# Two-dimensional DFT and squared-ReLU block: a new plan for the side work of the first sequence, and two joins moved between the halves of a front

## The chip, the cores and the metric

The kernel runs on one core of one Trainium2 chip. The metric is the time of one execution in microseconds (us) on the device; lower is better. The engines are named as in the profile: PE is TensorE (matrix products), DVE is VectorE, ACT is ScalarE, POOL is GpSimd, SP is SyncE, which here only issues DMAs.

## The reference

```python
X = np.fft.fft(np.fft.fft(x, axis=1), axis=2).real   # x: 8 x 3008 x 256, float32
h = X.reshape(24064, 256) @ w_in                     # w_in: 256 x 2048
r = np.maximum(h, 0.0)
out = (r * r) @ w_out                                # w_out: 2048 x 256
```

So each of 8 sequences (b) of 3008 rows goes through a DFT over its rows and one over its 256 columns, of which the real part is kept, and then through two dense layers with a squared ReLU between.

## The kernel before

The column DFT is folded into w_in (G1, G2), so that the first layer reads the row DFT directly. By symmetry a sequence needs only 1505 frequencies: Pt and Qt hold the cosine and sine parts, and one pair of products gives hP and hQ, whose sum and difference are the first layer at a frequency and at its mirror. The frequencies are cut into 6 blocks of 252 (the last has 246), the hidden width into 8 pairs of slices (j = 0 to 7). One (block, j) is a **step**; a sequence has 48 steps, and steps are numbered through all 8 sequences (i, here mostly modulo 48).

In step i, in this order in the program:

- `front`: PE computes hP and hQ into two PSUM tiles of the pool "h", which has two buffers. DVE makes `he` from hP (two instructions, L1017), then g from he and hQ (L1019, L1020).
- `pending` work of a gathering, then **folds** and **composites** (below), then stores of results.
- the second layer for a pair of earlier steps, with fewer products by a Winograd-like scheme: an F group of 12 products (`first_half`, odd i) or an S group of 8 (`second_half`, even i). A product appears as two matmul instructions. Their operands are g and the 12 sums s, which POOL makes (L1039 to L1041 for even steps, L1049 to L1056 for odd ones).
- ACT's relu and square of g (L1024, L1027), and POOL's sums of it.

A block ends with a **gathering**: F and S products lie in six PSUM tiles (F0 to F2, S0 to S2), which DVE joins into the result c in `upper` and `lower` (one step after the last F group) and `joins` (two steps after, behind that step's front). S1 and S2 share a pool with two buffers, so the next block's S products can use S1's buffer only when the joins have read it.

Beside this, the row DFT of sequence b + 1 is computed while sequence b runs. It is a list of pieces with costs in us: **folds** (`fold_later`), which add and subtract mirrored rows and columns of x: R (rows), C (columns), both (parities), order (a shuffle), even and odd (butterflies), twice_even, twice_turned and twice_odd. Most copy one operand with ACT into a "spare" tile of the PSUM pool "h", so that DVE reads only one operand from SBUF; **composites** (`even` and `odd` of `dft_ops`), which are 8 small matmuls (pd, L743, L840, L866) into a tile of the same pool "h", put into an F or S group after its second product, and DVE joins of their halves. The column 128 of x for sequences 1 to 7 goes through its own small folds in the first sequence (`fold_columns`: begin, order, odd, even, odd_sums, twice_even, twice_odd) and its own composites (`dft_ops(None)`), whose result is stored to e_dram and read back in windows.

How the list is spread: in sequences 2 to 7 `pieces` takes up to two folds in a step, while their costs fit in ROOM[j] and the work is behind its due amount (`spent`, paced over the sequence); a composite goes into the step's F or S group when due (`piece_beside`). In the first sequence `first_pieces` does the same with CAPACITY and BESIDE, from a list that `ahead` and `woven` put together: folds, column work, table rearrangements (`part_table`) and composites in one order. Steps with j = 2 and 3 take none. The first sequence starts with a written-out order of tokens (ORDER) for its steps 0 to 9, in which the weights are still being prepared; the planner runs from step 10 (PLAIN) on.

x tiles are loaded by SP into three buffers, each next load issued by the fold R that frees one; the 56 small loads of column 128 (`load_columns`, L454) are issued six per step.

Of the kernel before, what the change touches and what calls it, by code (L numbers as in the profile page):

```python
# [84 lines left out]
def kernel(  # L85
# [321 lines left out]
    def make_turn():  # L407
        c, z = (turn[0:ROWS2, a, BY_AC:BY_AC + 1] for a in range(2))
        for a, (u, v, op) in enumerate(((c, z, ALU.add), (c, z, ALU.subtract), (z, c, ALU.subtract))):
            to = turn[0:ROWS2, a, BY_BD:BY_BD + 1]  # L410
            tt(out=to, in0=u, in1=v, op=op)
            nc.scalar.mul(to, to, 0.5 ** 0.5)

# [43 lines left out]

    def scale_columns():
        nc.scalar.mul(xe, xe, 2.0)

    def fold_columns():
# [12 lines left out]
        def begin():  # L474
            assert not COLUMNS
            scale_columns()
            s = hp.tile([P, 2, NL, NE], F32, name="es", tag="es", bufs=1)
            gt(out=s, in0=xe[:, 0::2], in1=xe[:, 1::2], op=ADD)
            for kp in range(2):
                gt(out=we[:, :, kp], in0=s[:, 0], in1=s[:, 1], op=SUB if kp else ADD)  # L480
# [9 lines left out]
        def even():  # L490
            nc.scalar.copy(a, we[r, first, 0])
            pair_up(we[r, first, 0], we[r, other, 0], a)
# [10 lines left out]
        def twice_even():  # L503
            nc.scalar.copy(one, we[r, 2:3, 0])
            for i, (u, k) in enumerate(((7, SIN), (5, LESS))):
                nc.scalar.mul(f[:, i], we[r, u, 0], by(BY_AB, k))
            for u in (5, 7):
                nc.scalar.mul(we[r, u, 0], we[r, u, 0], by(BY_AB, COS))
            pair_up(we[r, 2:3, 0], we[r, 4:5, 0], one)
            gt(out=we[r, 5:8:2, 0], in0=we[r, 5:8:2, 0], in1=f, op=ADD)  # L510

        def twice_odd():
            nc.scalar.copy(pair, we[r, v, 1])
            pair_up(we[r, v, 1], we[r, w, 1], pair)

        return [(0.1, begin), (0.3, order), (0.1, odd), (0.1, even), (0.1, odd_sums), (0.1, twice_even), (0.1, twice_odd)]

# [59 lines left out]
    def spare(r):  # L577


        return psh.tile([P, 2 * D], F32, name="sp", tag="h")[r]  # L580

    def fold_later(b):

# [11 lines left out]
        def rows_of(t):  # L595
            r = rows(t)

            def f():
                v, p, k = xt[b, t], spare(r).rearrange("p (i d) -> p i d", i=2), ordered.index(t)
                nc.scalar.copy(p, v[r, 1:3])  # L600
                if b == 1:
                    for u in ordered[k + (k > 0):k + 2]:
                        difference(u)
                fs[t] = next_sums()
                tt(out=fs[t][r, :, 0:D], in0=v[r, 0::3], in1=p, op=ADD)
                if b > 1:
                    fd[t] = fp.tile([P, 2, D], F32, name="fd", tag="fd")
                    tt(out=fd[t][r], in0=v[r, 0::3], in1=p, op=SUB)
                load_later(LATER.index((b, t)) + NX)

            return 0.7 if b == 1 else 1.3, f
# [89 lines left out]
        R, C, both = rows_of, columns_of, parities_of  # L701
        if b == 1:
            one = [R(TWO), R(TWO + 1), C(TWO), R(0), C(TWO + 1), both(TWO, TWO + 1), R(1), C(0), order(TWO + 1), C(1),
                   R(av), both(0, 1), even((TWO, TWO + 1)), odd(TWO, TWO + 1, BY_TWO)]
            two = [C(av), R(aw), R(bv), C(aw), both(av, aw), C(bv), order(aw), R(bw), even((av, aw)), odd(av, aw, BY_AC),
                   C(bw), both(bv, bw), order(bv), even((bv, bw)), odd(bv, bw, BY_BD)]
            return one, two + [(0.9, twice_even), (1.1, twice_turned), (1.4, twice_odd)]
# [295 lines left out]

    def front(b, k0, n, j):

# [9 lines left out]
        for h in range(2):  # L1015
            fc = j + NJ * h
            nc.vector.scalar_tensor_tensor(out=t[:, h, 0:n], in0=window[b, k0][:, 0:n], scalar=gE[:, fc:fc + 1],  # L1017
                                           in1=hP[:, h, 0:n], op0=ALU.mult, op1=ALU.add)
        tt(out=g[:, :, 0:n], in0=t[:, :, 0:n], in1=hQ[:, :, 0:n], op=ALU.add)  # L1019
        tt(out=g[:, :, n:2 * n][:, :, ::-1], in0=t[:, :, 0:n], in1=hQ[:, :, 0:n], op=ALU.subtract)  # L1020
# [95 lines left out]
    def gather(n, final):  # L1116
# [37 lines left out]
        def joins():  # L1154
            tt(out=o[:, 3::-2], in0=o[:, 3::-2], in1=S0[:, 0:2], op=ADD)
            tt(out=S0[:, 2], in0=S0[:, 2], in1=vt[:, 4], op=ADD)
            if not final:
                tt(out=S1[:, 1], in0=vt[:, 0], in1=S1[:, 1], op=SUB)
            tt(out=o[:, 2::3], in0=o[:, 2::3], in1=wide(S0[:, 2:3]), op=ADD)
            tt(out=o[:, 0], in0=o[:, 0], in1=S1[:, 2], op=ADD)  # L1160
            if not final:
                tt(out=o[:, 4], in0=o[:, 4], in1=S1[:, 1], op=ADD)

        return c, (early, upper, lower, back, joins)

# [41 lines left out]
    def ahead(b):  # L1207
        (_, start), *groups = dft_ops(b)
        tables = [(0.0, lambda tab=tab, t=t: part_table(tab, t)) for t in (TWO, ODD0) for tab in (cosT, sinT)]
        one, two = fold_later(b)  # L1210
        if b > 1:
            return one + two + [(0.0, start)] + groups
        head = [(0.0, start), *one[:3], (0.2, take_turn), *one[3:5], (0.5, make_turn), *one[5:9]]
        return (head + one[9:11] + woven(one[11:] + two[:5], fold_columns(), 1) + tables
                + woven(two[5:], dft_ops(None) + groups[0::2], 1) + groups[1::2])

    def woven(ops, others, each):

        out, others = [], list(others)
        for k in range(0, len(ops), each):  # L1220
            out += ops[k:k + each] + others[:1]
            del others[:1]
        return out + others

# [113 lines left out]
    per = len(BLOCKS) * NJ  # L1338
    side, spent, pace = [], 0.0, 0.0


    PLAIN = NJ + 2
    SHARE = (1.4, 2.3, 0.0, 0.0, 0.7, 1.6, 1.4, 1.6)
    FIRST = (1.6, 2.8, 0.0, 0.0, 0.9, 1.9, 1.6, 1.9)

    BESIDE = (2.2, 2.9, 0.0, 0.0, 1.7, 2.4, 2.2, 2.4)
    CAPACITY = (1.8, 2.8, 0.0, 0.0, 1.2, 2.2, 1.8, 2.2)
    ROOM = (1.6, 2.4, 0.0, 0.0, 1.0, 1.8, 1.6, 1.8)

    def share(i):  # L1350
        return 0.0 if i < PLAIN + 2 else FIRST[i % NJ] if i < per else SHARE[i % NJ]

    late = []

    def free_pieces():
        while late:
            late.pop(0)()
        while side and not side[0][0]:
            side.pop(0)[1]()
# [13 lines left out]

    def first_pieces(j):


        nonlocal spent
        room, hook = CAPACITY[j], None
        while side:
            t, f = side[0]  # L1380
            if spent + t / 2 > 0 or t > room + (0.6 if f in beside else 0.3) or f in beside and (hook or late):
                break
            if (f in beside or hook) and t + CAPACITY[j] - room > BESIDE[j]:
                break
            side.pop(0)
            if not t:
                late.append(f)
                continue
            spent, room = spent + t, room - t
            if f in beside:  # L1390
                hook = (2, f)
            else:
                f()
        return hook

    def piece_beside():
# [17 lines left out]
    ).split()  # L1414
    rounds = {"2": round_win(2, raw["in", 2])}
    loaded, freed = [], set()
    made = {}
# [20 lines left out]

    finished, pending = [], []

# [14 lines left out]
    def step(token):  # L1455
# [10 lines left out]
        elif what == "et":  # L1466
            made["et"]()
        elif what == "lc":
            load_columns(4)
# [42 lines left out]
    i = 0  # L1512
    spent, pace = 0.0, sum(t for t, _ in side) / sum(share(k) for k in range(per - 2))
    load_more()
    for token in ORDER:
        step(token)
    for i in range(PLAIN, len(steps) + 7):
        if i < len(steps):
            b, k0, n, j = steps[i]
            if i % per == 0:  # L1520
                assert not side
                side = ahead(b + 1) if b + 1 < B else []
                spent, pace = 0.0, sum(t for t, _ in side) / sum(share(i + k) for k in range(per - 2))
            if j == 2 and i + NJ < len(steps):
                load_window(*steps[i - 2 + NJ][:3])
            made["g", i] = g = front(b, k0, n, j)
            if i == PLAIN:
# [9 lines left out]
        if i < len(steps) and share(i):  # L1537
            spent -= pace * share(i) * (1.0 if i >= per else 1.08)
            if i < per:
                hook = first_pieces(j)  # L1540
            else:
                pieces()
                hook = (2, piece_beside)
# [5 lines left out]
        if at >= NJ and at < len(steps):  # L1549
            b_, k0_, n_, j_ = steps[at]  # L1550
            q = j_ // 2
            if not last_half:
                first_half(q, n_, made["g", at], made["g", at + 1], made["s", group], hook)
                if q == NJ // 2 - 1:
                    final = at + 2 == len(steps)
                    c_, ops = gather(n_, final)
                    gather_next = ops[0]
                    pending += [(i + 1, ops[1])] + ([] if final else [(i + 2, ops[3])]) + [(i + 2, ops[4])]
                    lower = (i + 1, ops[2])
                    finished += [(i + 3 + k if final else i + 4 + 2 * k, b_, k0_, n_, s_, c_, final)  # L1560
# [11 lines left out]
        free_pieces()  # L1572
        load_columns(6)


# [61 lines left out]
```

## Time and profile before

| | us |
|---|---|
| three runs | 1895.47, 1895.70, 1895.86 |
| median | 1895.7 |
| profiled execution | 1896.75 |
| its span, first to last instruction | 1895.0 |
| PE, DVE, POOL, ACT busy | 1865.4, 1474.3, 1465.5, 1082.3 |

The profile is of one execution. Busy time counts an engine's instructions, not its waits. A line of the view of waits names the waiting engine, tile and line, then what it waited for, then total us, times and the longest. A row of a timeline gives start, duration, engine, line, operation, output and inputs, shape and count, and in brackets the idle time before it and what ended it. The chain of waits follows the work that ended last back through the program.

### The profile page before, as it was taken

The page shows a single profiled execution, that of the slowest core. Times are in us where ns is not written, and L with a number is a line of the kernel's source. Part 1 is how long each engine was busy: PE and PEld are TensorE (multiplying, and loading weights), DVE is VectorE, ACT ScalarE, POOL GpSimd, SP SyncE. Part 2 cuts the span into 40 slices and gives each one's busy share as a digit, 9 for nine tenths or more (in the row PEclk, how much of TensorE's full clock was granted, in tenths as well). Part 3 has the DMA queues.
Part 4 walks back from the last instruction along what each step waited for, and adds up shares of the span by engine and source line. Part 5 has one row for each costly group of instructions (what it writes and reads, how often), then busy time and mean ns, then how long its engine had stood idle before and what let it go on. Part 6 is the DMA issues. An engine that isn't in the chain of part 4 may idle for free.

```text
span 1895.0 us, 34082 instructions
## 1 busy us (share of the span) xinstructions
PE 1865.4 (98%) x11408; PEld 1755.4 (93%) x11408; DVE 1474.3 (78%) x3483; ACT 1082.3 (57%) x1614; POOL 1465.5 (77%) x2138
## 2 busy tenths in 40 slices
PE   9998999999999999999999999999999999999998
PEld 7678999999999999999999999999999999999998
DVE  7787887888778887888778787787877888766665
ACT  5866555656455654566556564565645656445453
POOL 4388778878788877878778887788778878787886
PEclk9999999999999999999999999999999999999999
DMA  7441101110021000111011110111001100000000
GB/s 196 117 55 37 24 15 45 45 34 17 18 56 40 24 20 23 47 40 28 23 31 31 48 29 15 32 45 48 15 15 45 39 15 19 16 23 15 20 20 22
DMA packets 151310, 68.46 MB, mean 36 GB/s; under 512 B 131143, under 2 KB 142881, under 8 KB 151136
## 3 DMA queue, kind: packets, MB, share of 16 engines
q1 hardware_dynamic: 150590, 65.74, 14.1%
q8 instruction: 91, 1.49, 0.3%
q14 instruction: 83, 0.68, 0.1%
q0 software_dynamic: 416, 0.43, 0.1%
q10 hardware_dynamic: 130, 0.12, 0.0%
HBM read 41.54 MB, written 24.69 MB: 35 GB/s over the span
## 4 chain that ended last, share of the span: by engine, by line
PE 82%; DVE 11%; DMA 2%; POOL 2%; ACT 2%; issue 1%; SPq 1%; DVEq 0%; POOLq 0%; ACTq 0%
PE F L1074 30%; PE S L1074 19%; PE hP L1013 15%; PE hQ L1013 14%; DVE he L1017 2%; DMA xt<-in_x_dram 2%; PE pd L866 1%; DVE g L1019 1%; DVE g L1020 1%; PE pd L743 1%; PE pd L840 1%; ACT sp L667 1%; DVE vt L1143 0%; DVE wsum L390 0%; SPq L454 0%
## 5 line engine op out<-in xcount | busy, mean ns | idle before, releaser
L1024 ACT ACTIVATE g<-g 128x1008 f32<-128x1008 f32 (+1 forms) x384 | 399.4, 1040 | 312.4 <-DVE g L1020 304.3
L1017 DVE SCALAR_TENSOR_TENSOR he<-ew,gE,hP 128x252 f32<-128x252 f32 (+1 forms) x748 | 321.4, 471 | 295.9 <-PE hP L1013 295.9
L1027 ACT ACTIVATE g<-g 128x1008 f32<-128x1008 f32 (+1 forms) x384 | 399.4, 1040 | 12.0
L1013 PE MATMUL hP<-Pt,G 128*128 128x252 f32 (+1 forms) x1496 | 381.3, 378 | 10.9 <-DVE w L669 6.3
L1013 PE MATMUL hQ<-Qt,G 128*128 128x252 f32 (+3 forms) x1496 | 380.0, 377 | 1.0 <-DVE g L1020 0.3
L1074 PE MATMUL F<-s,wsum 128*128 128x168 f32 (+1 forms) x1504 | 337.4, 306 | 0.0
L1049 POOL TENSOR_TENSOR s<-g 128x168 f32<-128x168 f32 (+1 forms) x188 | 101.7, 541 | 282.7 <-ACT g L1027 279.4
L1013 PEld LDWEIGHTS hQ<-Qt,G 128*128 128x128 f32 (+1 forms) x1496 | 281.7, 190 | 40.9 <-issue 2.4
L1074 PE MATMUL F<-g,wout 128*128 128x168 f32 (+1 forms) x1504 | 305.7, 305 | 0.0
L1013 PEld LDWEIGHTS hP<-Pt,G 128*128 128x128 f32 x1496 | 265.7, 190 | 33.0 <-ACT sp L654 4.3
L1019 DVE TENSOR_TENSOR g<-he,hQ 128x504 f32<-128x504 f32 (+1 forms) x374 | 253.3, 677 | 47.0 <-PE hQ L1013 3.8
L1074 PE MATMUL S<-s,wout 128*128 128x168 f32 (+1 forms) x1504 | 281.3, 306 | 0.1
L1074 PE MATMUL S<-s,wsum 128*128 128x168 f32 (+1 forms) x1504 | 275.0, 305 | 0.0
L1074 PE MATMUL F<-g,wsum 128*128 128x168 f32 (+1 forms) x1504 | 275.0, 305 | 0.0
L1020 DVE TENSOR_TENSOR g<-he,hQ 128x504 f32<-128x504 f32 (+1 forms) x374 | 250.5, 670 | 0.0
L1074 PEld LDWEIGHTS F<-s,wsum 128*128 128x128 f32 x1504 | 248.8, 190 | 0.3 <-issue 0.3
L1074 PEld LDWEIGHTS F<-g,wsum 128*128 128x128 f32 x1504 | 240.5, 190 | 8.1
L1074 PEld LDWEIGHTS S<-s,wsum 128*128 128x128 f32 x1504 | 240.4, 190 | 8.2 <-issue 0.2
L1074 PEld LDWEIGHTS F<-g,wout 128*128 128x128 f32 x1504 | 240.6, 190 | 0.0
L1074 PEld LDWEIGHTS S<-s,wout 128*128 128x128 f32 x1504 | 232.1, 190 | 0.7 <-POOL s L1056 0.3
L1052 POOL TENSOR_TENSOR s<-s 128x336 f32<-128x336 f32 (+1 forms) x188 | 168.9, 898 | 14.7
L1055 POOL TENSOR_TENSOR s<-s 128x336 f32<-128x336 f32 (+1 forms) x188 | 168.8, 898 | 14.7
(229 smaller groups left out, 2503.7 us busy)
## 6 DMA issues: line engine op xcount, KB each, us to landing
out_dram<-os SPq DMA_DIRECT2D x376, 56.0 KB
xt<-in_x_dram SPq DMA_DIRECT2D x39, 384.0 KB
xt<-in_x_dram SPq DMA_DIRECT2D x63, 128.0 KB
ew<-e_dram SPq DMA_DIRECT2D x39, 126.0 KB
out_dram<-os SPq DMA_DIRECT2D x288, 7.0 KB
raw<-in_moe_w_in_dram SPq DMA_DIRECT2D x16, 256.0 KB
raw<-in_moe_w_out_dram SPq DMA_DIRECT2D x16, 256.0 KB
xt<-in_x_dram SPq DMA_DIRECT2D x2, 512.0 KB
```

Source lines behind the costliest of these rows:

```text
L667: nc.scalar.mul(p[:, c0:c1], x[half, 1, c0:c1], by(i, a))
L743: nc.tensor.matmul(ps[0:w.shape[-1]], w, part_of(cosT if lone_e else tab, t)[0:rows, kp, PLACE[t]:PLACE[t] + NC[kp][c]], start=t == ts[0] ...
L1013: nc.tensor.matmul(to[:, h, 0:n], w[:, fs], v[:, ks], start=h == 0, stop=True, skip_group_check=True)
L1017: nc.vector.scalar_tensor_tensor(out=t[:, h, 0:n], in0=window[b, k0][:, 0:n], scalar=gE[:, fc:fc + 1], in1=hP[:, h, 0:n], op0=ALU.mult, op ...
L1019: tt(out=g[:, :, 0:n], in0=t[:, :, 0:n], in1=hQ[:, :, 0:n], op=ALU.add)
L1020: tt(out=g[:, :, n:2 * n][:, :, ::-1], in0=t[:, :, 0:n], in1=hQ[:, :, 0:n], op=ALU.subtract)
L1024: act(g[:, :, 0:2 * n], g[:, :, 0:2 * n], AF.Relu)
L1027: act(g[:, :, 0:2 * n], g[:, :, 0:2 * n], AF.Square)
L1049: gt(out=s[:, 11], in0=b2[:, 0], in1=b1[:, 0], op=SUB)
L1052: gt(out=s[:, 4:6], in0=s[:, 4:6], in1=s[:, 10:11].to_broadcast([P, 2, tb]), op=SUB)
L1055: gt(out=s[:, 6:9:2], in0=s[:, 2:4], in1=s[:, 6:8], op=ADD)
L1074: nc.tensor.matmul(acc[nm][:, slot, 0:tb], w, v, start=q == 0 and nm not in begun, stop=q == NJ // 2 - 1, skip_group_check=True)
```

## The change

It has four parts.

1. First sequence: composites leave the list. They have a list of their own, each with the number of folds that must have been drawn and the step from which it may come, and go one at a time into even steps that then take no fold; folds go into odd steps (and into even ones while no composite may come), as many as fit in CAPACITY[j] + 0.2, without pacing. The first two differences of x rows (POOL) move into the written-out order (token df).
2. The column work, take_turn, make_turn and the table rearrangements are put at the ends of fixed steps (11 to 23), and nearly all of the column work is given to GpSimd: xe's doubling, copies and products that ACT did, and make_turn's three adds that DVE did, whose three scalings on ACT become one.
3. In all sequences the last joins of a gathering (o[:, 0] and o[:, 4]) move from the end of `joins` into the next step's front, between he and g.
4. ROOM for j = 6 is 1.5 instead of 1.6.

```diff
     def make_turn():
...
-            tt(out=to, in0=u, in1=v, op=op)
-            nc.scalar.mul(to, to, 0.5 ** 0.5)
+            gt(out=to, in0=u, in1=v, op=op)
+
+    def scale_turn():
+        nc.scalar.mul(turn[0:ROWS2, :, BY_BD], turn[0:ROWS2, :, BY_BD], 0.5 ** 0.5)
...
         def begin():
-            scale_columns()
+            gt(out=xe, in0=xe, in1=xe, op=ADD)
...
         def even():
-            nc.scalar.copy(a, we[r, first, 0])
+            nc.gpsimd.tensor_copy(a, we[r, first, 0])
...
         def twice_even():
-            nc.scalar.copy(one, we[r, 2:3, 0])
+            nc.gpsimd.tensor_copy(one, we[r, 2:3, 0])
             for i, (u, k) in enumerate(((7, SIN), (5, LESS))):
-                nc.scalar.mul(f[:, i], we[r, u, 0], by(BY_AB, k))
+                gt(out=f[:, i], in0=we[r, u, 0], in1=by(BY_AB, k).to_broadcast([HALF2, NE]), op=ALU.mult)
             for u in (5, 7):
-                nc.scalar.mul(we[r, u, 0], we[r, u, 0], by(BY_AB, COS))
+                gt(out=we[r, u, 0], in0=we[r, u, 0], in1=by(BY_AB, COS).to_broadcast([HALF2, NE]), op=ALU.mult)
...
         def twice_odd():
-            nc.scalar.copy(pair, we[r, v, 1])
+            nc.gpsimd.tensor_copy(pair, we[r, v, 1])
...
-        return [(0.1, begin), (0.3, order), (0.1, odd), (0.1, even), (0.1, odd_sums), (0.1, twice_even), (0.1, twice_odd)]
+        return {18: (begin,), 20: (order,), 21: (odd, even), 22: (odd_sums,), 23: (twice_even, twice_odd)}
...
-                if b == 1:
-                    for u in ordered[k + (k > 0):k + 2]:
+                if b == 1 and k:
+                    for u in ordered[k + 1:k + 2]:
                         difference(u)
...
+            beginning.extend(lambda t=t: difference(t) for t in ordered[:2])
...
-    def front(b, k0, n, j):
+    def front(b, k0, n, j, middle):
...
             nc.vector.scalar_tensor_tensor(out=t[:, h, 0:n], ...)
+        if middle:
+            middle()
         tt(out=g[:, :, 0:n], in0=t[:, :, 0:n], in1=hQ[:, :, 0:n], op=ALU.add)
...
             tt(out=o[:, 2::3], in0=o[:, 2::3], in1=wide(S0[:, 2:3]), op=ADD)
+
+        def last_joins():
             tt(out=o[:, 0], in0=o[:, 0], in1=S1[:, 2], op=ADD)
             if not final:
                 tt(out=o[:, 4], in0=o[:, 4], in1=S1[:, 1], op=ADD)
...
     def ahead(b):
...
+        start()
+        tables = {k: (lambda tab=tab, t=t: part_table(tab, t),)
+                  for k, (tab, t) in zip((13, 14, 15, 16), ((tab, t) for t in (TWO, ODD0) for tab in (cosT, sinT)))}
+        extra.update({PLAIN + 1: (take_turn, make_turn), **tables, 17: (scale_turn,),
+                      **fold_columns()})
+        e, (n0, m0, n1, m1, store_e) = groups[0::2], dft_ops(None)
+        ready = len(one)
+        composites.extend([(ready, 0, e[0]), (ready, 0, e[1]), (0, 26, n0), (0, 26, m0), (0, 26, n1), (ready, 0, e[2]),
+                           (0, 26, (m1[0], lambda: (m1[1](), store_e[1]()))), (ready, 0, e[3]),
+                           *((len(one + two), 0, o) for o in groups[1::2])])
+        return one + two
...
-    ROOM = (1.6, 2.4, 0.0, 0.0, 1.0, 1.8, 1.6, 1.8)
+    ROOM = (1.6, 2.4, 0.0, 0.0, 1.0, 1.8, 1.5, 1.8)
...
+    def first_pieces(i, j):
+        nonlocal drawn
+        room = CAPACITY[j]
+        after, since, (_, f) = composites[0] if composites else (0, per, (0.0, None))
+        if drawn >= after and i >= since and (j % 2 == 0 or not side):
+            composites.pop(0)
+            return 2, f
+        while side and side[0][0] <= room + 0.2:
+            t, f = side.pop(0)
+            f()
+            drawn, room = drawn + 1, room - t
...
-        'f9a sq8 f9b d9a cm8 sc2b d9b sc0b rl9 hi9 su2b sq9 bk7 cm9 '
+        'f9a sq8 f9b df d9a cm8 sc2b d9b sc0b rl9 hi9 su2b sq9 bk7 cm9 '
...
-            made["g", i] = g = front(b, k0, n, j)
+            made["g", i] = g = front(b, k0, n, j, between.pop(i, None))
...
                     pending += [(i + 1, ops[1])] + ([] if final else [(i + 2, ops[3])]) + [(i + 2, ops[4])]
+                    if final:
+                        pending.append((i + 2, ops[5]))
+                    else:
+                        between[i + 3] = ops[5]
...
         load_columns(6)
+        for f in extra.pop(i, ()):
+            f()
```

CAPACITY is (1.8, 2.8, 0, 0, 1.2, 2.2, 1.8, 2.2) for j = 0 to 7. The costs of the first sequence's folds are 0.7 for R, 0.8 for C and order, 1.5 for both, 0.7 for even of one pair, 0.9 for odd and twice_even, 1.1 for twice_turned and 1.4 for twice_odd, in the order that `fold_later` gives (`one`, then `two`).

More of the change, by code (lines that the diff above doesn't have):

```diff
@@ L456, in load_columns @@
         del COLUMNS[:count]
-    def scale_columns():
-        nc.scalar.mul(xe, xe, 2.0)
     def fold_columns():
@@ L580, in spare @@
         return psh.tile([P, 2 * D], F32, name="sp", tag="h")[r]
+    beginning = []
     def fold_later(b):
@@ L1162, in joins @@
                 tt(out=o[:, 4], in0=o[:, 4], in1=S1[:, 1], op=ADD)
-        return c, (early, upper, lower, back, joins)
+        return c, (early, upper, lower, back, joins, last_joins)
     def store(b, k0, n, s, c, final):
@@ L1208, in ahead @@
         (_, start), *groups = dft_ops(b)
-        tables = [(0.0, lambda tab=tab, t=t: part_table(tab, t)) for t in (TWO, ODD0) for tab in (cosT, sinT)]
         one, two = fold_later(b)
@@ L1212, in ahead @@
             return one + two + [(0.0, start)] + groups
[L1213 to L1223, printed above, removed]
+        start()
[9 more added lines that the diff above has]
+        return one + two
     pieces = [fold(t) for t in range(NT)]
@@ L1338 @@
     per = len(BLOCKS) * NJ
-    side, spent, pace = [], 0.0, 0.0
+    side, spent, pace, drawn = [], 0.0, 0.0, 0
+    composites, extra = [], {}
     PLAIN = NJ + 2
     SHARE = (1.4, 2.3, 0.0, 0.0, 0.7, 1.6, 1.4, 1.6)
-    FIRST = (1.6, 2.8, 0.0, 0.0, 0.9, 1.9, 1.6, 1.9)
-    BESIDE = (2.2, 2.9, 0.0, 0.0, 1.7, 2.4, 2.2, 2.4)
     CAPACITY = (1.8, 2.8, 0.0, 0.0, 1.2, 2.2, 1.8, 2.2)
-    ROOM = (1.6, 2.4, 0.0, 0.0, 1.0, 1.8, 1.6, 1.8)
+    ROOM = (1.6, 2.4, 0.0, 0.0, 1.0, 1.8, 1.5, 1.8)
     def share(i):
-        return 0.0 if i < PLAIN + 2 else FIRST[i % NJ] if i < per else SHARE[i % NJ]
-    late = []
+        return 0.0 if i < PLAIN + 2 else SHARE[i % NJ]
     def free_pieces():
-        while late:
-            late.pop(0)()
         while side and not side[0][0]:
@@ L1372, in pieces @@
             spent, room, count = spent + t, room - t, count - 1
[L1374 to L1394, printed above, removed]
+    def first_pieces(i, j):
[9 more added lines that the diff above has]
+            drawn, room = drawn + 1, room - t
     def piece_beside():
@@ L1437, in rows_at @@
                 store_upper()
-    finished, pending = [], []
+    finished, pending, between = [], [], {}
     def back_at(i):
@@ L1467, in step @@
             made["et"]()
+        elif what == "df":
+            for f in beginning:
+                f()
         elif what == "lc":
@@ L1512 @@
     i = 0
-    spent, pace = 0.0, sum(t for t, _ in side) / sum(share(k) for k in range(per - 2))
     load_more()
@@ L1520 @@
             if i % per == 0:
-                assert not side
+                assert not side and not composites
                 side = ahead(b + 1) if b + 1 < B else []
@@ L1537 @@
         if i < len(steps) and share(i):
-            spent -= pace * share(i) * (1.0 if i >= per else 1.08)
+            spent -= pace * share(i)
             if i < per:
-                hook = first_pieces(j)
+                hook = first_pieces(i, j)
             else:
@@ L1573 @@
         load_columns(6)
+        for f in extra.pop(i, ()):
+            f()
 _INS = ['x', 'moe_w_in', 'moe_w_out', 'cos_s', 'sin_s', 'cos_d', 'sin_d', 'alt_d']
```

## The prediction, made before the changed kernel was run

> **What bounds the kernel now.** I read the page first.
>
> ```profile
> span 1895.0 us, 34082 instructions
> PE 1865.4 (98%) x11408; PEld 1755.4 (93%) x11408; DVE 1474.3 (78%) x3483; ACT 1082.3 (57%) x1614; POOL 1465.5 (77%) x2138
> ```
>
> TensorE is busy for 98%, so the change can only win what lies between its products. The chain of waits gives the full pitch:
>
> ```profile
> 321.07 3.42 PE F L1074 x24
> ...
> 330.17 3.42 PE F L1074 x24
> ...
> 470.95 2.88 PE F L1074 x20
> 481.84 2.88 PE F L1074 x20
> ```
>
> Two steps (fronts, 24 F and 16 S products) take 9.10 us where nothing waits; with two composites in them 10.89, in the narrower last block 8.97 and 10.72, so a composite costs about 0.88. In the first sequence the F group of step 11 starts at 102.22, that of step 47 at 293.87: 191.65 us. Without waits it would be 18 x 9.10, less 0.4 for the narrower last block, plus 12 x 0.88: 174.0. So 17.7 us are lost there. The waits of TensorE in 102 to 300 us say where:
>
> ```profile
> PE hP L1013 <- DVE w L669: 3.4, 1, 3.4
> PE pd L743 <- DVE g L1020: 3.2, 3, 1.2
> PE hP L1013 <- DVE w L638: 1.7, 1, 1.7
> PE hP L1013 <- DVE sc L623: 1.4, 2, 0.8
> PE pd L866 <- DVE g L1020: 0.9, 1, 0.9
> PE hP L1013 <- DVE g L1020: 0.9, 1, 0.9
> ```
>
> All wait for DVE to free one of the two PSUM buffers "h". Fronts, spares of the folds and composites take them in turn: a composite (pd) behind a fold in the same step waits for the front's g instead of its he. The largest wait has its root in DVE's timeline:
>
> ```profile
> 151.17 0.42 DVE L575 TENSOR_TENSOR w<-sp,w 94x256 f32<-94x256 f32 x1
> 156.03 0.01 DVE L484 LOAD_MASK_SELECT we<-we  x1 [4.44 <-POOL we L480]
> ```
>
> The shuffle of the columns stands in DVE's queue in step 20, ahead of the next front; `begin`, which it needs, stands on GpSimd behind 8 sums. The pitch of that pair is 14.18 instead of 9.10: 5.1 lost, more than the 3.4 waited, since the next front's products run at 2.02 and 1.57 us instead of 1.01.
>
> Sequences 2 to 7 repeat every 227.12 us. Ideal is 24 x 9.10 - 0.5 + 8 x 0.88 = 224.9, so 2.2 are lost in each. By the pitch of each pair of F starts, against its composites, they are at step 12 (0.11), 16 (0.36), 28 (0.36), 30 (0.72), 36 (0.37) and 44 (0.4). The waits after 300 us:
>
> ```profile
> PE hP L1013 <- DVE w L669: 2.9, 6, 0.5
> PE pd L743 <- DVE he L1017: 1.2, 6, 0.2
> ```
>
> The first is step 30 (two folds, `odd` 0.9 + `even` 0.7, in a short S step); the second step 44, where the front's he starts behind the joins. Sequence 8, with no folds, has 9.10 in every pair.
>
> **The first sequence, step by step.** Where the folds come follows from their costs and CAPACITY + 0.2: R(TWO), R(TWO+1) in step 12, three folds in 13, both in 14, three in 15, two in 16, two in 17, odd in 20, three in 21, two in 23, three each in 25, 29 and 33, one each in 37 and 39. Composites stand alone in steps 22, 24, 28, 30, 32, 36, 38, 40, 41, 44, 45, 46.
>
> *What goes.* Step 20: the shuffle now stands at the step's end and `begin` two steps earlier on GpSimd; 5.1. Composites no longer share a step with folds: the pd waits for g, 3.2 + 0.9, and with refilling 5 by the pitches of their pairs (12.86, 12.07, 12.16, 11.07). Steps 13 to 16: make_turn's three DVE adds, of one column each, took 2.80 us in step 14 and now are on GpSimd; pitches 10.55 and 11.08 show 3.4 lost.
>
> *What stays or comes.* Durations by rows: R is 0.59 on ACT and 0.68 on DVE, C 0.73 and 0.75, both 1.05 and 1.42, odd 1.57 and 0.87, even 0.35 and 0.83; a front's g is done 1.35 after hQ, an F group lasts 3.42. Queued by that: step 12 (two R in an S step: the buffer for hP comes with the first R's add, at 111.1 instead of g's 110.53) makes hP wait 0.5; 14, both, 0.3; 17, ACT full with the table copies (0.85 to 1.2 each), 0.5; 29, odd's mix done 3.9 after hQ, 0.55; 33 the same with twice_even, 0.65; the shuffle waits up to 1 us for begin, 0.5 on TensorE; small ones 0.4. Together 3.4, with GpSimd's 0.5 (below) 3.9; waits of 12.0 in the view made 17.7 lost (products refill slowly after each), so I take 1.4 times it: 5.5. Gain 17.7 - 5.5 = 12.
>
> *Queues that are passed.* SP: tile 1's load stays behind the six column loads (issued 116.05, landed 120.2 by GpSimd's wait at 120.37); tile av's now follows at once, ahead of eight stores, which end some 0.5 later; a table copy of step 14 reuses their buffer, up to 0.7 on ACT, half of which step 15 hides. take_turn's nine ACT copies, 0.94, pass to step 11, where ACT has 0.9 idle. The last column load was issued at 139.3, `begin` would start about 148. The column store moves from step 31 to 38, three steps ahead of the composite that overwrites its source (O00, step 41).
>
> *GpSimd.* Moved onto it: xe's doubling (224 elements; 112 take 0.42 and 336 0.90, so 0.66), three copies and four products of at most 21 columns at 0.2 to 0.22, three adds of turn at 0.2: 2.7 in all. Two differences (1.27 each) go to 90 to 94 us, where it idled 4.16. The sums take 5.92 in an odd and 1.98 in an even step, 7.9 of 9.1. From tile 1's landing at 120.2 it then works without a gap: one difference, sums of 13 done at 127.5; with one difference each in 15 and 16, sums of 17 at 146.1; with begin (1.64) in 18 and two differences in 21, sums of 21 at 166.0; with the column's odd and even (1.5), odd_sums (0.27) and twice parts (2.2), sums of 25 at 186.0. Their last sum is wanted by the third S product, three steps on: at about 128, 146.9, 166.9 and 186.2. So it just keeps up; I take 0.5. Bounds: nothing, if sums start earlier; 3 us, if the small ones cost double or the tile lands 1.5 later.
>
> The trace's price for this work is 0.90 on GpSimd against 0.50 on DVE for 336 elements. The Trainium skill (GPSIMD Engine Reference, section 4.1 Engine selection) speaks against such moves: two-input work is about 2 times slower there than on DVE. By it xe's doubling would take an estimated 0.76 (twice 0.38, between DVE's 0.32 for 168 and 0.50 for 336), and the gain would fall by 0.1.
>
> The three adds of turn took 144, 861 and 1940 ns on DVE. The Trainium skill (SBUF — State Buffer, section Who interferes with whom) has a DVE instruction with two SBUF inputs blocked by a GpSimd instruction that reads SBUF. By it the 2.8 are won whole and no new GpSimd instruction can hold the folds, whose second input is in PSUM; the trace agrees in that C's two adds stay at 0.41 and 0.42.
>
> **Last joins between the halves.** In the step after joins, DVE now does he (0.86) first, then two joins (0.56), then g. In step 20 of the third sequence, L1159 leaves DVE at 616.75 and hP ends at 616.63: he starts 0.48 earlier, and g at 618.2 as before. So hP's buffer comes 0.5 earlier and hQ's is not later. Step 44 wins 0.35 (its pd wanted he), 28 0.25 (ACT's four products start earlier). New is a wait: S1's buffer is read by the last join, now done at 616.75 + 0.78 (both he) + 0.24 + 0.32 = 618.09, and the next S1 product (k = 3) is due at 617.32 + 0.855 = 618.18; behind it in TensorE's queue stand five S products and the next front. The trace has 0.05 to 0.15 from DVE's end to TensorE's start: so between 0 and 0.07 per gathering, 46 times; I take 0.03: 1.4 us in all.
>
> **ROOM 1.5 in j = 6.** In sequences 2 to 7 step 30 then takes odd alone (0.65 won), everything behind moves on: twice_odd to step 37, the composites to 38 to 41 and 44 to 47; step 36's 0.34 goes too. New small waits 0.15. The last composite ends about 3.8 us into step 47's 4.3, before hP of the next sequence.
>
> Per sequence 0.25 + 0.65 + 0.34 + 0.35 - 0.15 - 0.2 = 1.24; six of them 7.4, less 0.3 in sequences 1 and 8: 7.
>
> **Sum.** 12 + 7 = 19. The profiled execution took 1896.75 (span 1895.0); the median is 1.05 below. 1896.75 - 19 = 1877.75, so a median of 1876.7.
>
> **Rivals.** *A, GpSimd comes last in the first sequence*: for it, the gapless 65 us above with 1 us to spare; against, its 33 us of idle time in 102 to 300, 30.3 of them for ACT. Then 6 of the 12 stay: 1882. 0.14. *B, S1 waits for real*: 0.15 to 0.2 x 46 = 8: 1885. 0.10. *C, slower*: the same place, but he doesn't pass the joins' chain: if he starts at 617.23 as before, the last join ends at 618.57, and each of 46 S groups waits 0.44 to 0.54, 20 to 25 us; the 3.6 of steps 28 and 44 are not won either. 1876.7 - 1.4 + 3.6 = 1878.9, and so 1899 to 1904. It decides from a wait of (1895.7 - 1878.9) / 46 = 0.37. Against it, the end of hP at 616.63 and DVE free at 616.75. 0.10. *D, the new plan of the first sequence frees nothing*, since x tiles, ACT (26 us of work in 25 us, steps 11 to 17) or three spares in a row set the pace: only the 7 of the later sequences, 1888.7, or with S1 waits nothing seen. 0.06, of it 0.02 for no change.
>
> **Numbers.** The forecast has 0.60, with 1872 to 1881 as its own range. A measurement can tell 0.2%, 3.8 us. The range takes in A and B, and goes to 1871.5 for a first sequence 3 better and S1 at nothing, to 1887 for A with half of B; C, D and the tails stay out. Faster 0.60 + 0.14 + 0.10 + 0.04 = 0.88, same 0.02, slower 0.10.
>
> **What would show it.** Right: F groups of step 17 near 132, of 31 near 200, of 47 near 282; no wait of DVE for POOL we above 1 us; pd waits below 0.3; pitch of steps 29 and 30 9.1 instead of 9.82; pitch of steps 19 and 20 still 9.10. Wrong: waits of S for DVE L1162 or L1160 (B, C), waits of S for POOL s L1056 before 190 us (A), waits of hP for sc or w of over 1 us in steps 12 to 33 (D), or composites in 46 and 47 that make the next sequence's first front wait.

## The result, and the profile after

| | median, us | ratio to before, with 95% interval |
|---|---|---|
| before | 1895.8 | |
| changed kernel | 1871.1 (1870.5 to 1871.5) | 0.9868 (0.9848 to 0.9887) |

One further run of the changed kernel, at a granted clock of 0.752 instead of 0.998, took 2419.8 and is left out (with it the median would be 1871.3). The gain is 24.7 us. Faster was right; a gain of 19 was forecast, and the time lies 0.4 below the range's low end of 1871.5.

The head of the page after:

```profile
span 1869.3 us, 34067 instructions
PE 1854.7 (99%) x11408; PEld 1755.2 (94%) x11408; DVE 1466.6 (78%) x3480; ACT 1082.9 (58%) x1604; POOL 1465.4 (78%) x2149
```

The span is 25.7 shorter with the same 11408 matmuls. GpSimd has 11 instructions more and the same busy time. The view of waits, TensorE alone, in 100 to 300 us:

```profile
PE hP L1015 <- DVE w L670: 1.4, 2, 0.7
PE hP L1015 <- DVE fs L606: 1.4, 1, 1.4
PE hQ L1015 <- DVE g L1024: 0.3, 1, 0.3
```

The line of hQ lies ahead of the F group of step 11. From that group on, eight lines with 12.1 us (the prediction shows the six largest) became two with 2.8. No composite (pd) waits any more there, and no S product waits for GpSimd. What is left is where the prediction queued it: `fs` in step 12 (two R in an S step), `w` behind odd's mix in steps 29 and 33. After 300 us TensorE's waits are one line, 3.1 us at the very end, which stood there before as well; both lines shown of before (hP for w, pd for he) are gone. DVE's wait for `begin`, in the waits of DVE:

```profile
DVE we L483 <- POOL we L479: 0.2, 1, 0.2
```

It was 4.44. The starts of the F groups:

| F group of step | before | after | forecast |
|---|---|---|---|
| 11 | 102.22 | 101.25 | |
| 17 | 134.08 | 130.39 | near 132 |
| 31 | 211.09 | 199.04 | near 200 |
| 47 | 293.87 | 279.72 | near 282 |
| period of sequences 2 to 7 | 227.12 | 225.17 | 225.9 |

The 25.7 are 13.2 from the F group of step 11 to that of step 47, 11.6 behind it, and 0.97 ahead of it. The last is not shown to be the change's: in the ten profiles of the experiments that group starts between 101.28 and 101.76, at 101.49 and 101.76 in the two with the old first sequence.

In the later sequences the excess over the pitch without waits went, by step, at 12 from 0.11 to 0, at 28 from 0.36 to 0, at 30 from 0.72 to 0, at 36 from 0.36 to 0; at 44 the pitch fell by 0.46, from 10.25 to 9.79 (the prediction had put the whole excess there at 0.4); 16 keeps 0.36, and 32 goes from 0.03 to 0.1.

### The profile page after: what moved, and what is told of

Its sections match the earlier page's. It is cut to its first block, busy times and chain, and to the rows that moved or that the text cites. A ratio compares the mean times of both kernels' runs of the same rounds, so it can differ in the third digit from the quotient of the medians.

```text
span 1869.3 us, 34067 instructions
## 1 busy us (share of the span) xinstructions
PE 1854.7 (99%) x11408; PEld 1755.2 (94%) x11408; DVE 1466.6 (78%) x3480; ACT 1082.9 (58%) x1604; POOL 1465.4 (78%) x2149
## 4 chain that ended last, share of the span: by engine, by line
PE 95%; DVE 3%; ACT 1%; issue 0%; POOL 0%; DMA 0%; DVEq 0%; POOLq 0%; ACTq 0%
PE F L1078 33%; PE S L1078 23%; PE hP L1015 17%; PE hQ L1015 17%; PE pd L745 2%; PE pd L868 1%; PE pd L842 1%; PE pg L345 0%; DVE wsum L390 0%; PE mA L1107 0%; PE mB L1107 0%; DVE he L1001 0%; DVE he L1019 0%; DVE g L1003 0%; PE ph L986 0%
## 5 line engine op out<-in xcount | busy, mean ns | idle before, releaser
L1031 ACT ACTIVATE g<-g 128x1008 f32<-128x1008 f32 (+1 forms) x384 | 399.4, 1040 | 12.1
```

Source lines behind the costliest of these rows:

```text
L1031: act(g[:, :, 0:2 * n], g[:, :, 0:2 * n], AF.Square)
```

## The experiments

The part that each kernel undoes or adds is given against the changed kernel unless it says otherwise. In the views below, lines of code are up to three higher or lower than in the changed kernel.

### The parts alone

**First sequence alone** (parts 1 and 2):

```diff
-    ROOM = (1.6, 2.4, 0.0, 0.0, 1.0, 1.8, 1.5, 1.8)
+    ROOM = (1.6, 2.4, 0.0, 0.0, 1.0, 1.8, 1.6, 1.8)
...
-                    if final:
-                        pending.append((i + 2, ops[5]))
-                    else:
-                        between[i + 3] = ops[5]
+                    pending.append((i + 2, ops[5]))
```

> The changed kernel without its parts 3 and 4: the last joins are back at the end of joins, ROOM for j = 6 is 1.6 again. Theory: the three parts add up, and the first sequence alone wins what its F starts show (191.65 before, 178.47 after, and step 11 starts 0.97 earlier): 13 to 14 us, about 1882. Rival: parts 3 and 4 also won in the first sequence, since the joins in step 35 delay he of step 36: then this wins only 9 to 11, about 1886.

Measured: 1884.9, ratio 0.9941 (0.9926 to 0.9956). The F groups of steps 11 and 47 are 179.8 apart, 11.9 less than before: the term of 12 was right for this part. Part 3 gives the other 1.3 of the 13.2: without it the pairs of F starts from 19, 27, 35 and 43 take 9.47, 10.21, 10.26 and 10.27 instead of 9.11, 10.06, 10.00 and 9.81. The median gained 11.0 only; in this profile two of the later periods are 0.3 and 0.4 longer than 227.12, for which the edit gives no reason.

**Last joins alone** (part 3 with nothing else), against the kernel before:

```diff
+        if middle:
+            middle()
         tt(out=g[:, :, 0:n], in0=t[:, :, 0:n], in1=hQ[:, :, 0:n], op=ALU.add)
...
+        def last_joins():
             tt(out=o[:, 0], in0=o[:, 0], in1=S1[:, 2], op=ADD)
...
+                        between[i + 3] = ops[5]
...
```

> The kernel before with part 3 alone (last joins between he and g). Theory: the joins fill the pause of 0.22 us that DVE has between he and g, so g comes 0.22 earlier, and steps 12, 28, 36 and 44 of sequences 2 to 7 lose their 0.11 + 0.36 + 0.37 + 0.40 = 1.24: 7.4 us, 8 with step 36 of the first sequence, about 1888; a period of 225.9 instead of 227.12; no wait for S1. Rival, as the prediction had it: g stays, step 12 keeps its wait, S1 costs 0.03 at each gathering: 0.95 - 0.2 per period, about 4 us in all, 1891.5.

Measured: 1887.9, ratio 0.9956 (0.9941 to 0.9971). The waits of TensorE after 300 us, without the one at the end:

```profile
PE hP L1013 <- DVE w L669: 2.9, 6, 0.5
```

Step 30's line is as before, pd's wait for he is gone, and no S product waits. The period is 225.82, 1.30 less: steps 12, 28, 36 and 44 lost 0.11, 0.36, 0.36 and 0.47.

**ROOM alone** (part 4 with nothing else), against the kernel before:

```diff
-    ROOM = (1.6, 2.4, 0.0, 0.0, 1.0, 1.8, 1.6, 1.8)
+    ROOM = (1.6, 2.4, 0.0, 0.0, 1.0, 1.8, 1.5, 1.8)
```

> The kernel before with part 4 alone (ROOM 1.5 for j = 6). Theory: step 30 loses its 0.75, step 36 its 0.37 since its composite moves to 38, step 32 gains 0.11, step 44 keeps its wait behind the joins: 1.0 in each of six periods, 6 us, about 1890, a period of 226.1. Rival: the composites of steps 46 and 47 reach into the next sequence's first front: less than 4 us.

Measured: 1890.9 (1888.9 to 1891.5), ratio 0.997 (0.9958 to 0.9981). Here the other line is left:

```profile
PE pd L743 <- DVE he L1017: 1.4, 6, 0.4
```

Steps 30 and 36 are clean, 12, 28 and 44 stay as they were. In the trace the period is 226.13, 0.99 less (0.72 + 0.36, less 0.07 or 0.08 in step 32). The median's 5.0 is nearer to the prediction's 0.84 per sequence (0.65 + 0.34 - 0.15) six times, but these runs spread over 2.6 us, so the trace decides.

The three gains of the medians, 11.0 + 8.0 + 5.0 = 24.0, come close to the change's 24.7, which is partly chance, since step 36's 0.36 is in two of them. By the traces a later sequence wins 1.30 + 0.99 - 0.36 = 1.93 from parts 3 and 4, and 1.95 was measured. The old first sequence also varies from run to run: the pair of its largest wait takes 14.17 in the profile of before, 15.66 and 15.63 in these two kernels.

### The place of the last joins

**Joins behind g** in the front, instead of ahead of it:

```diff
-        if middle:
-            middle()
         tt(out=g[:, :, 0:n], in0=t[:, :, 0:n], in1=hQ[:, :, 0:n], op=ALU.add)
         tt(out=g[:, :, n:2 * n][:, :, ::-1], in0=t[:, :, 0:n], in1=hQ[:, :, 0:n], op=ALU.subtract)
+        if middle:
+            middle()
```

> The changed kernel with the last joins behind g instead of ahead of it. Theory: the next block's S products wait for S1's buffer, which the last join now frees some 1.4 us after the third S product's place (601.96 in the third sequence): 46 times 1 to 1.5 us, 45 to 70 us slower than the changed kernel, 1916 to 1941, with waits of S for DVE's join line; this is the price that the rival of a slower kernel spoke of. Rival: S1's buffer does not gate the S products: the same time within 3 us.

Measured: 1894.6, ratio 0.9993 (0.9984 to 1.0003): 23.6 more than the changed kernel, 0.6 in five of the six gatherings of a later sequence. The pair from step 43 stays at 9.79: its S group holds a composite ahead of the product that waits elsewhere. The wait of rivals B and C exists, then, when the joins come late enough:

```profile
PE S L1078 <- DVE c L1168: 13.1, 36, 0.6
```

But it is not where the prediction put it. TensorE's timeline in step 20 of the third sequence, and the row of DVE that it waits for:

```profile
607.09 0.45 PE L1078 MATMUL S<-s,wsum 128*128 128x168 f32 x2
607.38 1.02 PE L1078 MATMUL S<-s,wout 128*128 128x168 f32 x6
608.23 0.73 PE L1078 MATMUL S<-s,wsum 128*128 128x168 f32 x4
609.32 0.55 PE L1078 MATMUL S<-s,wsum 128*128 128x168 f32 x2 [0.36 <-DVE c L1168]
...
608.95 0.32 DVE L1168 TENSOR_TENSOR c<-c,S 128x168 f32<-128x168 f32 x1
```

A product is two instructions, so 12 of them are six products: three into S0, three into S1. The seventh, S2's first, waits for the join that ends at 609.27. S1's products had begun 1.3 us before that end. So the buffer that the last join frees is taken by the next S2, due three products (0.855) later, and not by the next S1, as the prediction and the account of the kernel before have it. That, and not a smaller price of a wait, is why this kernel lies below the forecast made for it.

**Only the second of the two joins** between the halves:

```diff
+            tt(out=o[:, 0], in0=o[:, 0], in1=S1[:, 2], op=ADD)
+
         def last_joins():
-            tt(out=o[:, 0], in0=o[:, 0], in1=S1[:, 2], op=ADD)
             if not final:
```

> The changed kernel with only o[:, 4] between he and g; o[:, 0] is back in joins, ahead of he. So he starts 0.24 later than in the changed kernel, 0.24 earlier than before, and DVE is busy without a pause either way. Theory (what counts is that the pause of 0.22 between he and g is filled, so that g comes earlier): the same as the changed kernel within 1 us, 1871 to 1872, periods of 225.2. Rival (what counts is how early he comes): about half of part 3's gain is lost, 4 us, 1875.

Measured: 1874.0, ratio 0.9884 (0.9869 to 0.9898), between the two expectations. Step 12's pitch is 9.10, as with both joins, though he starts 0.24 later than there: what counts in step 12 is that g is earlier. Step 28 keeps 0.13, and step 44 has 10.01 instead of 9.79: there he's earlier start counts. So the gain has both sources.

### GpSimd and the columns

**`begin` late**, in step 20 with the shuffle behind it, two steps later than in the changed kernel:

```diff
-        return {18: (begin,), 20: (order,), 21: (odd, even), 22: (odd_sums,), 23: (twice_even, twice_odd)}
+        return {20: (begin, order), 21: (odd, even), 22: (odd_sums,), 23: (twice_even, twice_odd)}
```

> The changed kernel with begin in step 20, right ahead of the shuffle in program order, instead of in step 18. Theory: DVE comes to the shuffle near 148.7, GpSimd has done sums of 20 near 155.5 and begin near 157, so DVE waits some 8 us, hP of step 22 comes 8 to 9 us late, and with refilling the kernel is 8 to 11 us slower than the changed one: 1879 to 1882. Rival: as before the change, the wait costs at most the 5.1 of that pair: 1876.

Measured: 1879.9, ratio 0.9915 (0.9899 to 0.9932). The wait is back, longer than in the kernel before, and the pair that holds it takes 19.34 instead of 10.00. First TensorE's wait, then DVE's for `begin`:

```profile
PE hP L1015 <- DVE fs L606: 8.8, 2, 7.4
DVE we L483 <- POOL we L479: 8.3, 1, 8.3
```

That confirms the chain of the largest wait of before (GpSimd's begin, DVE's shuffle, the next buffer "h").

**The small work back on ACT and DVE**, at the new steps: make_turn's three adds on DVE, xe's doubling, the copies and the products on ACT.

```diff
-            gt(out=to, in0=u, in1=v, op=op)
+            tt(out=to, in0=u, in1=v, op=op)
+            nc.scalar.mul(to, to, 0.5 ** 0.5)
...
-            gt(out=xe, in0=xe, in1=xe, op=ADD)
+            nc.scalar.mul(xe, xe, 2.0)
...
```

> The changed kernel with the column work and make_turn on the engines of before (ACT's doubling, copies and products, DVE's three adds with ACT's three scalings), at the new fixed steps. GpSimd has 2.7 us less work. Theory: GpSimd keeps up in the changed kernel without a wait of TensorE for it, so nothing is won; DVE's three adds of one column are held by GpSimd's instructions for up to 2.8 us in steps 11 and 12: 1 to 3 us slower, 1872 to 1875. Rival: GpSimd's 75 us without a pause hold TensorE somewhere: 1 to 3 us faster, 1868 to 1870.

Measured: 1873.5, ratio 0.9882 (0.9867 to 0.9896). One line of TensorE's waits differs from the changed kernel, where it has 1.4:

```profile
PE hP L1016 <- DVE fs L607: 2.8, 1, 2.8
```

The pair that holds it takes 13.67 instead of 10.76; the others of the first sequence stay as they were to 0.03. The adds stand ahead of he in DVE's queue, and the wait is 1.4 longer. First DVE's adds and TensorE's front in this kernel, then that front in the changed one:

```profile
107.55 1.27 DVE L411 TENSOR_TENSOR turn<-turn 96x1 f32<-96x1 f32 x3
111.65 2.05 PE L1016 MATMUL hP<-Pt,G 128*128 128x252 f32 x4 [2.76 <-DVE fs L607]
113.49 1.66 PE L1016 MATMUL hQ<-Qt,G 127*128 127x252 f32 x4
```

```profile
110.20 1.12 PE L1015 MATMUL hP<-Pt,G 128*128 128x252 f32 x4 [1.38 <-DVE fs L606]
111.16 1.02 PE L1015 MATMUL hQ<-Qt,G 127*128 127x252 f32 x4
```

Behind the wait of 2.76 the products run slower: the granted clock is 0.53 in the 3.4 us from 111.6 on, and 1.00 behind the wait of 1.38. So of all that moved to GpSimd only make_turn's adds are worth time, 2.9 us of one pair (2.4 in the median): 1.4 of wait and 1.5 of slower products. On DVE these one-column adds took 145 to 862 ns here (144 to 1940 before) and on GpSimd 179 to 187 in the changed kernel; the one of 862 ends at 108.82, with a sum of GpSimd that ran from 107.91 to 108.81. That agrees with the Trainium skill (SBUF — State Buffer, section Who interferes with whom), which says that a DVE instruction with two SBUF inputs contends with a GpSimd instruction that reads SBUF. xe's doubling took 0.56 on GpSimd, less than the 0.66 that the prediction put down for it.

**More work for GpSimd**: two differences, which stand in step 21, done twice, 2.5 us.

```diff
-            gt(out=fd[t][r], in0=v[r, 0::3], in1=v[r, 1:3], op=SUB)
+            for _ in range(2 if t in (ODD0 + 2, ODD0 + 3) else 1):
+                gt(out=fd[t][r], in0=v[r, 0::3], in1=v[r, 1:3], op=SUB)
```

> The changed kernel with the two differences of step 21 (1.25 us each on GpSimd) done twice, 2.5 us more on GpSimd between sums of 20 and of 21. In the changed kernel sums of 25 end at 183.8 and are wanted by the third S product of step 28 at 184.4: 0.6 to spare, the least of all steps. Theory: GpSimd works without a pause there, so all but 0.6 comes back as waits of S for POOL s: 1.9 us, 2 to 3 with refilling, 1873.5 to 1874.5. Rival: GpSimd's 22% of idle time hides it: the same within 0.5 us.

Measured: 1873.8, ratio 0.9878 (0.9864 to 0.9891), 2.7 more than the changed kernel. A new line of waits stands in 100 to 300 us:

```profile
PE S L1079 <- POOL s L1061: 1.3, 1, 1.3
```

2.5 us of work leave a wait of 1.3: GpSimd had 1.2 to spare, where the prediction said 1 and the expectation 0.6. The pairs from steps 21, 23 and 25 take 10.30, 12.34 and 9.34 instead of 10.00, 10.14 and 9.11, 2.7 more. Beside the wait these are small delays of products ahead of it and behind it; the granted clock stays at 1.00 there.

### Which rule of the new plan counts

**Composites in the odd steps, beside the folds**, instead of even steps of their own:

```diff
-        if drawn >= after and i >= since and (j % 2 == 0 or not side):
+        hook = None
+        if j % 2 == 0 and i >= 22 and side:
+            return None
+        if drawn >= after and i >= since:
             composites.pop(0)
-            return 2, f
+            hook = 2, f
...
+        return hook
```

> The changed kernel with its seven composites of steps 22 to 38 moved into odd steps with folds (21, 23, 29, 31, 33, 37, 39); the folds stay in their steps, the even steps 22 to 38 are empty. All work is the same. Theory: a pd then takes the PSUM buffer that the second last fold frees: waits of 2.3 (step 21), 1.6 (23), 3.4 (29 and 33) and 0.85 (31, 37, 39), 13 us, with refilling 17, less 2 of waits that are there anyway: 1884 to 1888, and waits of pd for folds' adds (sc, fs, w) in the view. Rival: the engines have the same work and room in each pair of steps, so within 3 us of the changed kernel.

Measured: 1892.8, ratio 0.9981 (0.9971 to 0.999): 21.8 of the 24.7 are gone, and the time lies above the expectation's upper end of 1888. Composites wait behind the folds again, 14.6 us in all where 13 were expected. The two largest of five lines:

```profile
PE pd L745 <- DVE w L670: 7.1, 2, 3.6
PE pd L745 <- DVE fs L606: 2.9, 1, 2.9
```

Behind the two waits of 3.6 the granted clock is 0.67 and 0.50 for 3.4 us, so these cost more than their length. The F groups of steps 11 and 47 are 198.1 apart, above the 191.7 of before: with composites and folds in the same steps the new plan is worse than the old one. Keeping them in different steps is the core of part 1.

**A candidate**: odd as the last fold of its step, and ROOM 1.5 for j = 0 as well.

```diff
-            ... R(bw), even((av, aw)), odd(av, aw, BY_AC),
-                   C(bw), both(bv, bw), order(bv), even((bv, bw)), odd(bv, bw, BY_BD)]
-            return one, two + [(0.9, twice_even), (1.1, twice_turned), (1.4, twice_odd)]
+            ... R(bw), even((av, aw)), C(bw),
+                   odd(av, aw, BY_AC), both(bv, bw), order(bv), even((bv, bw)), (0.9, twice_even), odd(bv, bw, BY_BD)]
+            return one, two + [(1.1, twice_turned), (1.4, twice_odd)]
...
-    ROOM = (1.6, 2.4, 0.0, 0.0, 1.0, 1.8, 1.5, 1.8)
+    ROOM = (1.5, 2.4, 0.0, 0.0, 1.0, 1.8, 1.5, 1.8)
```

> A candidate: the changed kernel with two small changes. The fold odd comes last in steps 29 (behind C) and 33 (behind twice_even), so that hP of the next step waits for the fold ahead of it and only hQ for odd's long one; and ROOM is 1.5 for j = 0 too, so that step 16 of sequences 2 to 7 takes one C and step 17 the other. Theory: the waits of hP for w (0.7 twice, 2.1 by the pitches 11.01 and 10.19) go, and the 0.36 of step 16 in six sequences: 2.1 + 2.2 = 4.3 us less, 1867. Rival: odd last delays he of steps 30 and 34, and step 17, in which a gathering begins, passes the delay on: 2 us less or nothing, 1869 to 1871.

Measured: 1869.0, ratio 0.9851 (0.9837 to 0.9864), the lowest of all, 2.1 below the changed kernel; that is less than 0.2%, so it rests on the trace. There step 16 has lost its 0.36 in each of the six later sequences (2.2 us), which is ROOM's edit. The other edit wins less than it was meant to: hP's two waits of 0.7 are gone, but hQ now waits in the same two places, 0.55 and 0.37, by the profile for ACT:

```profile
PE hQ L1015 <- ACT g L1028: 0.9, 2, 0.6
```

The pairs from steps 29 and 33 take 10.88 and 9.94 instead of 11.00 and 10.18, and the first sequence as a whole is no shorter (178.9 against 178.5): two pairs ahead of it, whose work is unchanged, took 0.5 and 0.3 longer. Whether this edit is worth its 0.4 is left open.

## Why the prediction was right or wrong

| term | forecast | measured |
|---|---|---|
| first sequence, parts 1 and 2 | 12 | 11.9 in its trace, 11.0 in the median |
| first sequence, part 3 | 0 | 1.3 |
| last joins, each later sequence | 0.25 + 0.35 - 0.2 = 0.4 | 1.30 alone |
| ROOM, each later sequence | 0.84 | 0.99 alone in its trace, 5.0 / 6 = 0.84 in the median |
| both, each later sequence | 1.24 | 1.95 |
| last sequence and end | -0.3 for the first and the last | about -0.5 |

**Right: the first sequence.** The largest wait, the pd waits and make_turn went as worked out, and the losses that were to stay are there: with parts 1 and 2 alone 5.8 by the F starts (179.8 - 174.0) against 5.5, with part 3 4.5. That the sum comes so close is partly luck, since single terms were mis-sized in both directions. Step 12 lost 1.7 of its pair and was put down with 0.7: the 0.5 by which hP's wait grew is right (0.9 to 1.4), but the 0.9 that was there before was not counted among what stays. The shuffle and GpSimd cost next to nothing instead of 0.5 each. The one factor of 1.4 for slow refilling also covers two different cases: behind the largest wait of before the granted clock is 0.56 for 3.3 us, and that is why its pair lost 5.1 with 3.4 waited. The changed kernel has no wait that long in its first sequence, and the clock is 1.00 behind each.

**Right in kind: ROOM.** Steps 30 and 36 lost what they were to lose and a little more (0.72 and 0.36 against 0.65 and 0.34), and the new small wait, in step 32, costs 0.07 to 0.08 (0.15 forecast): 0.99 instead of 0.84.

**Wrong: the last joins.** The step that failed is "he starts 0.48 earlier, and g at 618.2 as before". The prediction took DVE's work as a plain sum, in which two joins ahead of he or behind he leave g where it was. DVE's timeline in step 20 of the third sequence, first of before, then of after (start, duration, engine, line, operation), shows that they don't:

```profile
616.75 0.32 DVE L1160 TENSOR_TENSOR c<-c,S 128x168 f32<-128x168 f32 x1
616.99 0.32 DVE L1162 TENSOR_TENSOR c<-c,S 128x168 f32<-128x168 f32 x1
617.23 0.86 DVE L1017 SCALAR_TENSOR_TENSOR he<-ew,gE,hP 128x252 f32<-128x252 f32 x2
618.22 0.68 DVE L1019 TENSOR_TENSOR g<-he,hQ 128x504 f32<-128x504 f32 x1
```

```profile
600.53 0.86 DVE L1019 SCALAR_TENSOR_TENSOR he<-ew,gE,hP 128x252 f32<-128x252 f32 x2
601.31 0.32 DVE L1166 TENSOR_TENSOR c<-c,S 128x168 f32<-128x168 f32 x1
601.55 0.32 DVE L1168 TENSOR_TENSOR c<-c,S 128x168 f32<-128x168 f32 x1
601.79 0.67 DVE L1023 TENSOR_TENSOR g<-he,hQ 128x504 f32<-128x504 f32 x1
```

Before, g starts 0.99 after he, though he's two instructions take 0.86: it reads what he writes and starts 0.13 after he's end. A join, which doesn't need he, starts 0.78 after he, 0.08 ahead of its end, and g after the joins likewise 0.08 ahead of theirs. (In `lower` two instructions in a row also read what the one ahead of each has written: they start 0.10 and 0.03 after its end, in the third sequence of before.) From the start of the first of these four instructions to g it was 0.24 + 0.24 + 0.99 = 1.47 before and is 0.78 + 0.24 + 0.24 = 1.26 after. The joins now fill a pause of 0.21 that DVE made between he and g. So g's end, hQ's buffer and ACT's start are earlier too, not only hP's: steps 12 and 28 lose all of their 0.11 and 0.36 instead of 0.25 together, step 36 loses its 0.36 by the joins as well as by ROOM, and the first sequence, where the buffers "h" are short, wins 1.3.

The second step that failed is S1's wait, 0.03 x 46 = 1.4 us: it is nothing. Its time was right (the last join ends at 601.87 where S begins at 601.11), its place was not: it is S2's first product, due at 601.11 + 6 x 0.285 = 602.82, that takes the buffer. There are 0.95 us to spare where the prediction had a wait of 0 to 0.07.

Of the 5.7 that the sum lacked by the traces (13.18 + 11.55 against 19), the two make up 3.8: 1.3 in the first sequence and, six times, 0.2 (S1) + 0.11 (step 12) + 0.11 (step 28). Another 1.7 is small sizes, six times 0.07 (step 30), 0.02 (36), 0.11 (44) and 0.08 (32), and 0.35 is one longer period that before had and after has not. The last sequence and the end took back 0.2 more than was written.

**The rivals.** A: GpSimd had 1.2 to spare in step 24 and is not last; with 2.5 us more it is, for 1.3. B and C: the wait is real, as the kernel with the joins behind g shows, but three products further on than either assumed. D: the first plan frees 11 by itself. The prices of B and C were worked out for a tight place that isn't there, and their chance of 0.20 pulled the range upward and left too little of it below.

## What to carry to other kernels

Where an instruction reads what the one ahead of it on its engine has just written, look in the timeline for the gap between them: independent work put there costs less than its own time. When two kinds of work take buffers from one small pool in turn, put them in different steps before trimming either. Look for the longest wait first: here only the longest ones also slowed the products behind them. A wait for a buffer is priced at the product that takes the buffer, so settle which one that is; moving the release on purpose until something waits shows it in one run.

## What the runs showed of the hardware

- DVE: 0.21 us between an instruction and one that needs its result, against one that doesn't (0.13 after the end against 0.08 ahead of it, with he and g as above; 0.10 and 0.03 after the end in `lower`).
- TensorE: behind waits of 0.7 to 1.8 us hP's four matmuls took 1.09 to 1.12 us (1.01 without a wait), at a granted clock of 1.00. Behind waits of 2.8 to 7.4 us they took 2.02 to 2.05, at 0.50 to 0.57 over the 3.4 us that followed (two profiles had 0.63 and 0.64 for another 3.4). A composite kept 1.00 behind a wait of 2.9 and had 0.67 and 0.50 behind two of 3.6. So a longer wait can cost much beyond its length: pairs with 3.4 waited took 14.17 and 15.66 instead of 9.10.
- One-column adds with both inputs in SBUF took 144 to 1940 ns on DVE, while GpSimd worked, and 179 to 187 ns on GpSimd.
